# Two pairs of the third attention summed unit by unit on VectorE, and its softmax sums joined without TensorE

## The chip, the cores and the metric

The kernel runs on one core of a Trainium2 chip. The metric is the device time of one execution in microseconds.

## The reference

The computation is a grouped-query attention over 8 batches (16 query heads, 4 key heads, 384 positions, head size 64), whose output goes through a hierarchical mixture of experts (4 groups of 4 experts, model width 1024, hidden width 1024). Cut to what matters:

```python
scores = scale * q @ k.T                       # per batch and head, 384 x 384
attn = exp(scores - max); attn /= attn.sum(-1) + 1e-9
x = (attn @ v) laid out as 3072 tokens x 1024
g = argmax(x @ w_group);  e = argmax(x @ w_expert[g])     # one expert per token
out = softmax_g[g] * softmax_e[e] * (relu(x @ w1[g, e]) @ w2[g, e])
```

## The kernel before

Each batch is one attention followed by one block. An attention has 24 units (4 groups of heads, 6 units of keys each). For unit u, TensorE makes the scores (L318), ScalarE their exponentials into a tile e of 128x768 (L324), and TensorE multiplies these with v into PSUM (L337), two units behind the scores. The result of a group is copied to xT by VectorE (L379).

The softmax sums are made beside that. GpSimd adds the tiles of two units (`pair`, L345), in place in the first of them, and VectorE reduces the sum with a transposing reduction (`reduce`, L354). `lags` says at which unit's tail a reduction is queued; in the third attention (b = 2) the reduction of pair u-2 stands in the tail of unit u, and the last one, of unit 23, in the block behind it. A unit in `apart` is not added: `pair` does nothing and `reduce` reduces both tiles, each into a slot of its own of `red3`. The list of the third attention is empty before.

The block behind an attention interleaves the expert layer of the batch before (`moe_h` L636, `ffn_y` L650) with the end of the softmax. `join_keys` adds the slots of each group: with equal numbers of slots it is one instruction (L407), otherwise one for each group. Then the sums of the 32-row strips must be added and spread over the partitions. There are two ways: `sums` does it with TensorE (L416) and two reciprocals on VectorE (L432); `sums_copied` does it on VectorE alone, with copies and additions (L441, L442), one reciprocal (L443) and eight copies (L447). The third batch uses `sums`, those after it `sums_copied`. Then `normalise` runs four times, each a transposing spread (L455) and a multiplication (L459). Behind that VectorE casts a small mean (L482), and TensorE makes the gate's logits (L474), the softmax of the gate follows, and the next attention.

In the block of b = 2 VectorE also runs the gate's softmax of batch 1 (L505 to L537) and its output weights (L614, L618), between `join_keys` and the sums. On GpSimd the same block queues a wait for the transposed q (L604), two weight loads, and three additions that sum v (L112 to L114).

Every engine works off its queue in the order of the program, which is written out by hand.

Of the kernel before, what the change touches and what calls it, by code (L numbers as in the profile page):

```python
# [18 lines left out]
def kernel(  # L19
# [14 lines left out]
    _, Hkv, _, _ = k.shape  # L34
# [12 lines left out]
    NU = Hkv * NC  # L47
# [20 lines left out]
    def ps_tile(which, shape=None, dtype=F32):  # L68
        if which == "x":
            which = f"o{1 - turn['o']}"  # L70
        else:
            turn[which] = 1 - turn[which]
            which += str(turn[which])
        return psum.tile(shape or [P, 2, 512], dtype, name="ps_" + which)
# [20 lines left out]
    def load_k(b, src=None):  # L95
        nc.gpsimd.dma_start(out=k_pad[:, D:(NK + 1) * D].rearrange("p (a n) -> p a n", n=NC * D),
                            in_=rows(k[b] if src is None else src))

    def load_q(b, src=None):
        qraw[b] = lpool.tile([P, KQ, NC * D], BF16, name="q_raw")  # L100
        nc.gpsimd.dma_start(out=qraw[b], in_=rows(q[b] if src is None else src))

    def load_v(b, src=None):
        vraw[b] = vpool.tile([P, NA, NC * D], F32, name="v_raw")
        nc.sync.dma_start(out=vraw[b], in_=rows(v[b] if src is None else src))

    def sum_v(b):
        t = gpool.tile([P, NA * D], BF16, name="vsum")
        s = gpool.tile([P, NA, NC // 2 * D], F32, name="vs")
        v_ = vraw[b]  # L110
        hn = NC // 2 * D
        nc.gpsimd.tensor_add(out=s, in0=v_[:, :, :hn], in1=v_[:, :, hn:])  # L112
        nc.gpsimd.tensor_add(out=s[:, :, :D], in0=s[:, :, :D], in1=s[:, :, D:2 * D])
        nc.gpsimd.tensor_add(out=t.rearrange("p (h d) -> p h d", d=D), in0=s[:, :, :D],  # L114
                             in1=s[:, :, 2 * D:])
        vsum[b] = t
# [285 lines left out]
    def join_keys(b, g0, g1):  # L402
        if b not in red:
            red[b] = gpool.tile([P, Hkv, 2, NB], F32, name="red", bufs=2)
        same = len(set(parts[b][g0:g1])) == 1
        for g, h in [(g0, g1)] if same else [(g, g + 1) for g in range(g0, g1)]:
            nc.vector.tensor_reduce(  # L407
                out=red[b][:, g:h].rearrange("p g t j -> p g (t j)"),
                in_=red3[b][:, g:h, :parts[b][g]].rearrange("p g c t j -> p g (t j) c"),
                axis=AX.X, op=ALU.add)  # L410

    def sums(b, g0, g1, which, tiles=False):
        sm = ps_tile(which)[:, :, :(g1 - g0) * 2 * NB]
        for r in range(2):
            if not tiles:
                nc.tensor.matmul(out=sm[:, r], lhsT=half32[:, r, :],  # L416
                                 rhs=red[b][:, g0:g1].rearrange("p g t j -> p (g t j)"),
                                 start=True, stop=True)
                continue
            rs = slice(r * H2, (r + 1) * H2)  # L420
            for t in range(2):
                nc.tensor.matmul(
                    out=sm[t * D:(t + 1) * D, r].rearrange("p (g t j) -> p g t j", t=2, j=NB)[:, :, t],
                    lhsT=half32[rs, r, t * D:(t + 1) * D], rhs=red[b][rs, g0:g1, t],
                    start=True, stop=True)
        if b not in inv:
            inv[b] = gpool.tile([P, KQ, NB], F32, name="inv", bufs=2)
        iv = inv[b][:, 2 * g0:2 * g1].rearrange("p (g r) j -> p r g j", r=2)
        sm = sm.rearrange("p r (g t j) -> p r g t j", t=2, j=NB)
        for t in range(2):  # L430
            ts = slice(t * D, (t + 1) * D)
            nc.vector.reciprocal(out=iv[ts], in_=sm[ts, :, :, t])  # L432
# [3 lines left out]
    def sums_copied(b, which):  # L436
        r_, sm = red[b], red3[b][:2 * Q, :, 4]
        sw = ps_tile(which)[:, 0, :Hkv * 2 * NB].rearrange("p (g t j) -> p g t j", t=2, j=NB)
        for r in range(2):
            lo, hi = slice(2 * r * Q, (2 * r + 1) * Q), slice((2 * r + 1) * Q, (2 * r + 2) * Q)  # L440
            nc.vector.tensor_copy(out=sw[lo], in_=r_[hi])  # L441
            nc.vector.tensor_add(out=sm[r * Q:(r + 1) * Q], in0=r_[lo], in1=sw[lo])  # L442
        nc.vector.reciprocal(out=sm, in_=sm)  # L443
        inv[b] = gpool.tile([P, KQ, NB], F32, name="inv", bufs=2)
        for r in range(2):
            for h in range(4):
                nc.vector.tensor_copy(out=inv[b][h * Q:(h + 1) * Q, r::2, :],  # L447
                                      in_=sm[r * Q:(r + 1) * Q, :, h // 2, :])
# [157 lines left out]
    def pick_w1(b):  # L606
        w1s[b] = fetch1(ers[b])
# [37 lines left out]
    def ffn_y(w2, hT, c, which, nhs=(0, 1), y=None):  # L645
        if y is None:
            y = ps_tile(which)
        for nh in nhs:
            for f in range(FQ):
                nc.tensor.matmul(out=y[:, nh, :], lhsT=hT[:, f, c * P:(c + 1) * P],  # L650
                                 rhs=w2[:, f, nh * HALF:(nh + 1) * HALF],
                                 start=(f == 0), stop=(f == FQ - 1))
        return y
# [19 lines left out]
    def moe_y(b, c, which):  # L673
        y_out(b, c, ffn_y(w2s[b], hTs[b], c, which))
# [6 lines left out]
    def before_attention(b):  # L681

        if b + 1 < B:
# [10 lines left out]
             for i in range(5)]  # L694
    at = {
        0: Attn(0, act_copies=(0, 1, 3),
                lags={5: [1], 6: [3], 8: [5], 10: [7], 12: [9], 14: [11], 18: [13], 21: [15],
                      22: [17]}),
        1: Attn(1, apart=(9, 11), act_copies=(2, 3), later=(7, 13, 15, 17), homes=homes,
                lags={18: [13], 19: [15], 20: [17], 22: [19], 23: [21]}),  # L700
    }
# [97 lines left out]
    def first_block():  # L799
        load_v(3)  # L800
        moe_y(0, 0, "s")
        sum_v(2)
        load_k(3)
        load_q(3)
        at[1].reduce(NU - 1)
        join_keys(1, 0, Hkv)
        y = ffn_y(w2s[0], hTs[0], 1, "s", (0,))
        sums(1, 0, Hkv, "o")
        ffn_y(w2s[0], hTs[0], 1, "s", (1,), y)
        y_out(0, 1, y)  # L810
        y = ps_tile("o")
        normalise(1, 0, "x")
        normalise(1, 2, "x")
        cast(1, 0)
        ffn_y(w2s[0], hTs[0], 2, "o", (0,), y)
        at[2] = Attn(2, later=(1,), lags={5: [1], 6: [3], **{u: [u - 2] for u in range(7, NU, 2)}})
        at[2].score(0)
        at[2].score(1)
        ffn_y(w2s[0], hTs[0], 2, "o", (1,), y)
        y_out(0, 2, y)  # L820
        normalise(1, 1, None, pool)
        normalise(1, 3, None, pool)
# [17 lines left out]
    def block(b):  # L840
        last = b == B - 1
        f = b - 1
        if b + 2 < B:
            load_v(b + 2)
        if not last:
            after_transposes(b + 1)
        pick_w1(b)
        pick_w2(b)
        if not last:
            sum_v(b + 1)  # L850
        if b + 2 < B:
            load_k(b + 2)
            load_q(b + 2)
        moe_h(f, 0, "s")
        at[b].reduce(NU - 1)
        join_keys(b, 0, Hkv)
        if b == 2:
            gate_softmax(1, state["gl"], False)()
            out_weights(1)
        moe_h(f, 2, "s")  # L860
        if b == 2:
            sums(b, 0, Hkv, "o")
        else:
            sums_copied(b, "o")
        normalise(b, 0)
        normalise(b, 1)
        moe_h(f, 4, "s")
        normalise(b, 2)
        moe_h(f, 6, "s")
        cast(b, 0)  # L870
        cast(b, 1)
        normalise(b, 3)
        moe_y(f, 0, "s")
        cast(b, 2)
        pt = ps_tile("o")
        y = ffn_y(w2s[f], hTs[f], 1, "s", (0,))
        vm = None if last else guess_mean(b + 1, pt)
        ffn_y(w2s[f], hTs[f], 1, "s", (1,), y)
        cast(b, 3)
        y_out(f, 1, y)  # L880
        gate_logits(b, pt)
        if not last:
            guess_logits(vm, guess_out(pt))
            at[b + 1] = Attn(b + 1)
            at[b + 1].score(0)
            at[b + 1].score(1)
        w = gate_softmax(b, gate_rows(pt, not last), not last)
        if not last:
            pick(b + 1)
            pick_index(b + 1)  # L890
            read_pick(b + 1)
        w()
        out_weights(b)
        y = ffn_y(w2s[f], hTs[f], 2, "o")
        if last:
            y_out(f, 2, y)
            return {}
        return {1: [do(y_out, f, 2, y, True)]}
# [148 lines left out]
```

## Time and profile before

| what | value |
|---|---|
| median of 3 runs | 359.56 us (358.8 to 362.1) |
| the profiled execution's own time | 359.14 us |
| its span | 357.2 us |
| TensorE busy (matmul) | 347.3 us, 97% |
| VectorE busy | 256.6 us, 72% |
| ScalarE busy | 225.1 us, 63% |
| GpSimd busy | 220.4 us, 62% |

The span is what the trace covers; the own time is 1.9 us longer. Times in the trace are microseconds from the span's start. The third attention runs from 73.5 to 95.6 us, its block to 119.4 us.

### The profile page before, as it was taken

What the parts mean: (1) busy time and instruction counts of PE and PEld (TensorE: products, weight loads), DVE (VectorE), ACT (ScalarE), POOL (GpSimd) and SP (SyncE); (2) the same over time, 40 slices, a digit from 0 to 9 for tenths busy, and PEclk for the clock granted to TensorE, in tenths of its full rate; (3) what the DMA queues carried; (4) which work ended last, traced back from release to release, by engine and by line L of the source; (5) the groups of instructions that cost most, each with busy time, mean ns of one, the idle gap of its engine ahead of it and who ended that gap; (6) DMA issues with size and microseconds to landing.
All of it is one profiled execution on the core that took longest, in us unless ns stands there. A gap on an engine that the chain in (4) does not pass through costs nothing.

```text
span 357.2 us, 9201 instructions
## 1 busy us (share of the span) xinstructions
PE 347.3 (97%) x3799; PEld 183.1 (51%) x3814; DVE 256.6 (72%) x521; ACT 225.1 (63%) x295; POOL 220.4 (62%) x172
## 2 busy tenths in 40 slices
PE   8999999999999999999999999999999999999993
PEld 4455565445555455544555554545545544555642
DVE  5797769767697777977679767886769676795031
ACT  5899935399536794378934598256963679444320
POOL 6879995869935598607984099902995059900000
PEclk9999999999999999999999999999999999999999
DMA  8999999799999999899989999899987991099924
GB/s 203 185 157 163 222 208 177 130 272 223 194 173 178 262 208 188 190 221 244 193 199 177 233 226 194 180 204 250 196 182 124 197 267 65 2 183 220 245 67 117
DMA packets 69486, 67.15 MB, mean 188 GB/s; under 512 B 37144, under 2 KB 49688, under 8 KB 69440
## 3 DMA queue, kind: packets, MB, share of 16 engines
q0 software_dynamic: 26640, 41.03, 66.3%
q1 hardware_dynamic: 42352, 24.94, 30.3%
q8 instruction: 32, 0.52, 0.6%
q10 hardware_dynamic: 448, 0.54, 0.5%
q14 instruction: 14, 0.11, 0.1%
HBM read 86.07 MB, written 12.58 MB: 276 GB/s over the span
## 4 chain that ended last, share of the span: by engine, by line
PE 83%; DVE 6%; POOL 5%; ACT 2%; issue 1%; POOLq 0%; DVEq 0%
PE ps_o L337 29%; PE ps_s L636 19%; PE ps_s L650 11%; PE ps_s L318 8%; PE ps_o L650 6%; PE ps_o L474 3%; POOL e L345 2%; ACT e L324 2%; PE ps_s L927 2%; POOL w L345 1%; PE ps_o L636 1%; DVE xT L459 1%; PE ps_o L927 1%; DVE e L455 1%; POOL xb L466 1%
## 5 line engine op out<-in xcount | busy, mean ns | idle before, releaser
L345 POOL TENSOR_TENSOR e<-e 128x768 f32<-128x768 f32 x91 | 162.7, 1825 | 74.6 <-PE ps_s L318 67.9
L324 ACT ACTIVATE e<-ps_s 128x768 f32<-128x768 f32 x187 | 147.6, 813 | 19.5 <-PE ps_s L318 17.4
L337 PE MATMUL ps_o<-e,v_raw 64*64 64x384 f32 x1496 | 149.1, 482 | 0.0
L354 DVE TRANSPOSE_TENSOR_REDUCE red<-e 128x24 f32<-128x768 f32 x95 | 91.4, 971 | 38.1 <-POOL e L345 38.1
L636 PE MATMUL ps_s<-xb,w 128*128 128x384 bf16 x480 | 80.1, 326 | 0.1
L337 PEld LDWEIGHTS ps_o<-e,v_raw 64*64 64x64 f32 x1496 | 55.3, 133 | 36.4 <-issue 29.0
L636 PEld LDWEIGHTS <-w 128*128 128x128 bf16 x512 | 49.4, 98 | 36.4 <-issue 4.5
L318 PE MATMUL ps_s<-qT,kT 64*64 64x384 bf16 x768 | 64.7, 328 | 0.3
L650 PEld LDWEIGHTS <-hT 128*128 128x128 bf16 x336 | 31.8, 98 | 38.8 <-issue 2.3
L640 ACT ACTIVATE hT<-ps_s 128x768 bf16<-128x768 f32 x23 | 18.6, 810 | 50.6 <-PE ps_s L636 47.2
L650 PE MATMUL ps_s<-w,hT 128*128 128x512 bf16 x217 | 49.4, 379 | 0.4
L318 PEld LDWEIGHTS <-kT 64*64 64x64 bf16 x768 | 24.3, 105 | 34.6 <-issue 32.6
L464 ACT CAST xb<-xT 128x768 bf16<-128x768 f32 x28 | 23.3, 832 | 10.0 <-DVE xT L459 9.8
L379 DVE COPY xT<-ps_o 128x768 f32<-128x768 f32 x26 | 24.0, 924 | 2.6 <-ACT xb L464 1.5
L455 DVE STREAM_TRANSPOSE e<-inv 128x768 f32<-128x768 f32 x26 | 25.2, 971 | 0.2
L650 PE MATMUL ps_o<-w,hT 128*128 128x512 bf16 x105 | 24.0, 379 | 1.1 <-issue 1.1
L459 DVE TENSOR_TENSOR xT<-xT,e 128x768 f32<-128x768 f32 x24 | 23.1, 961 | 0.8
L669 ACT ACTIVATE ot<-ps_s,we 128x1024 f32<-128x1024 f32 x14 | 15.6, 1114 | 8.6 <-PE ps_s L650 8.5
L495 DVE STREAM_TRANSPOSE gl<-ps_o 128x96 f32<-128x96 f32 x8 | 2.3, 283 | 16.8 <-PE ps_o L487 12.2
L643 ACT ACTIVATE hT<-ps_s 128x384 bf16<-128x384 f32 x14 | 6.1, 488 | 12.5 <-PE ps_s L636 12.5
L447 DVE COPY inv<-red 32x48 f32<-32x48 f32 x40 | 10.6, 265 | 0.6
L474 PEld LDWEIGHTS ps_o<-xT,wg 128*32 128x32 f32 x448 | 9.2, 110 | 3.7 <-DVE vm L482 1.7
(141 smaller groups left out, 227.3 us busy)
## 6 DMA issues: line engine op xcount, KB each, us to landing
w<-in_moe_w_dram POOLq DMA_DIRECT2D x16, 2048.0 KB, 21.9
out_dram<-ot SPq DMA_DIRECT2D x42, 256.0 KB, 7.1
q_raw<-in_q_dram POOLq DMA_DIRECT2D x7, 768.0 KB, 27.4
v_raw<-in_v_dram SPq DMA_DIRECT2D x7, 384.0 KB, 4.6
k_raw<-in_k_dram POOLq DMA_DIRECT2D x7, 192.0 KB, 24.4
out_dram<-ot SPq DMA_DIRECT2D x9, 128.0 KB, 2.7
w<-in_q_dram POOLq DMA_DIRECT2D x3, 192.0 KB, 6.3
w<-in_k_dram SPq DMA_DIRECT2D x2, 192.0 KB, 3.7
```

The source lines that it names most:

```text
L318: nc.tensor.matmul(out=sT[r * H2:(r + 1) * H2, s, :S], lhsT=kT[b][s * D:(s + 1) * D, key_block(b, s, g // 2, c), ks], rhs=qT[b][s * D:(s + ...
L324: nc.scalar.activation(e.rearrange("p t (s x) -> p s t x", s=2), sT[:, :, :S].rearrange("p s (t x) -> p s t x", t=2), ACT.Exp, scale=scale)
L337: nc.tensor.matmul(out=oT[t * D:(t + 1) * D, r, :S], lhsT=vraw[b][r * H2:(r + 1) * H2, g // 2, c * D:(c + 1) * D], rhs=self.e[u][r * H2:(r ...
L345: nc.gpsimd.tensor_add(out=self.e[u - 1], in0=self.e[u - 1], in1=self.e[u])
L354: nc.vector.tensor_reduce(out=red3[b][:, g, parts[b][g]].rearrange("p t j -> p (t j)"), in_=self.e[w].rearrange("p t (j x) -> p (t j) x", ...
L379: nc.vector.tensor_copy(out=dst, in_=src)
L455: nc.vector.transpose(out=rb.rearrange("p k (j x) -> p k j x", x=32), in_=inv[b][:, ks].unsqueeze(3).to_broadcast([P, 2, NB, 32]))
L459: eng.tensor_mul(out=x, in0=x, in1=rb)
L464: nc.scalar.copy(out=xb[b][:, ks, :], in_=xT[b][:, ks, :])
L474: nc.tensor.matmul(out=pt[32 * t:32 * t + 32, 0, :S // 4], lhsT=wg[:, head_pair(m), :], rhs=x[:, t], start=(m == 0), stop=(m == KQ - 1))
L636: nc.tensor.matmul(out=h[:, jj, :S], lhsT=w1[:, head_pair(m), (f0 + jj) * P:(f0 + jj + 1) * P], rhs=x[:, m, :], start=(m == 0), stop=(m == ...
L650: nc.tensor.matmul(out=y[:, nh, :], lhsT=hT[:, f, c * P:(c + 1) * P], rhs=w2[:, f, nh * HALF:(nh + 1) * HALF], start=(f == 0), stop=(f == ...
```

## The change

Two things change, both for b = 2. The pairs that end in units 15 and 21 get into `apart`: GpSimd doesn't add them, VectorE reduces their four tiles one by one, and two of the four groups then have four slots in `red3` in place of three. And the block no longer calls `sums` for b = 2 but `sums_copied`, as for the later batches.

```diff
-        at[2] = Attn(2, later=(1,), lags={5: [1], 6: [3], **{u: [u - 2] for u in range(7, NU, 2)}})
+        at[2] = Attn(2, apart=(15, 21), later=(1,), lags={5: [1], 6: [3], **{u: [u - 2] for u in range(7, NU, 2)}})
...
         moe_h(f, 2, "s")
-        if b == 2:
-            sums(b, 0, Hkv, "o")
-        else:
-            sums_copied(b, "o")
+        sums_copied(b, "o")
         normalise(b, 0)
```

## Rows read from the trace of the kernel before

**Rows 1.** The page: busy time of each engine, share of the span.
```profile
PE 347.3 (97%) x3799; PEld 183.1 (51%) x3814; DVE 256.6 (72%) x521; ACT 225.1 (63%) x295; POOL 220.4 (62%) x172
```

**Rows 2.** The chain that ended last, 90 to 165 us: start, length, what.
```profile
93.67 1.94 PE ps_o L337 x24
...
100.93 0.69 PE ps_o L416 x4
...
112.00 1.75 PE ps_s L650 x8
113.74 1.46 PE ps_o L474 x64
...
145.80 1.05 DVE inv L447
...
156.02 0.17 DVE vm L482
```

**Rows 3.** Timeline of TensorE, the gate's logits of the third and the fourth batch.
```profile
113.67 1.53 PE L474 MATMUL ps_o<-xT,wg 128*32 128x96 f32 x64
...
156.23 1.53 PE L474 MATMUL ps_o<-xT,wg 128*32 128x96 f32 x64 [0.27 <-DVE vm L482]
```

**Rows 4.** Timeline of VectorE, 80 to 114 us: start, length, instruction [idle before].
```profile
83.77 2.69 DVE L354 TRANSPOSE_TENSOR_REDUCE red<-e 128x24 f32<-128x768 f32 x3
...
90.51 0.98 DVE L354 TRANSPOSE_TENSOR_REDUCE red<-e 128x24 f32<-128x768 f32 x1 [0.81 <-POOL e L345]
92.28 0.98 DVE L354 TRANSPOSE_TENSOR_REDUCE red<-e 128x24 f32<-128x768 f32 x1 [0.80 <-POOL e L345]
93.18 0.92 DVE L379 COPY xT<-ps_o 128x768 f32<-128x768 f32 x1
94.07 0.98 DVE L354 TRANSPOSE_TENSOR_REDUCE red<-e 128x24 f32<-128x768 f32 x1
...
99.38 0.98 DVE L354 TRANSPOSE_TENSOR_REDUCE red<-e 128x24 f32<-128x768 f32 x1
100.39 0.48 DVE L407 TENSOR_REDUCE red<-red 128x96 f32<-128x288 f32 x1
100.79 0.15 DVE L505 TENSOR_REDUCE mx<-gl 128x3 f32<-128x12 f32 x1
...
103.86 1.51 DVE L432 RECIPROCAL inv<-ps_o 64x96 f32<-64x96 f32 x2
105.41 0.98 DVE L455 STREAM_TRANSPOSE e<-inv 128x768 f32<-128x768 f32 x1
...
113.12 0.16 DVE L482 CAST vm<-ps_o 128x2 bf16<-128x2 f32 x1
```

**Rows 5.** Timeline of GpSimd, 64 to 110 us.
```profile
77.95 21.39 POOL L345 TENSOR_TENSOR e<-e 128x768 f32<-128x768 f32 x12
104.33 0.18 POOL L604 COPY tok<-qT 1x1 bf16<-1x1 bf16 x1 [4.99 <-DMA qT<-q_raw]
...
106.76 1.54 POOL L112 TENSOR_TENSOR vs<-v_raw 128x384 f32<-128x384 f32 x1
```

**Rows 6.** Groups by form, `join_keys`: busy, mean ns of one, idle before.
```profile
L407 DVE TENSOR_REDUCE red<-red 128x96 f32<-128x288 f32 x6 | 2.9, 478 | 0.2
...
L407 DVE TENSOR_REDUCE red<-red 128x24 f32<-128x72 f32 x5 | 1.0, 213 | 0.0
```

**Rows 7.** Timeline of VectorE, 309 to 328 us, the last batch's `sums_copied`.
```profile
312.72 0.25 DVE L441 COPY ps_o<-red 32x96 f32<-32x96 f32 x1
...
314.64 1.52 DVE L447 COPY inv<-red 32x48 f32<-32x48 f32 x8
316.20 0.98 DVE L455 STREAM_TRANSPOSE e<-inv 128x768 f32<-128x768 f32 x1
```

**Rows 8.** Timeline of VectorE and of GpSimd, 134 to 162 us, the fourth batch.
```profile
145.36 2.98 DVE L447 COPY inv<-red 32x48 f32<-32x48 f32 x8
...
145.79 1.02 POOL L112 TENSOR_TENSOR vs<-v_raw 128x384 f32<-128x384 f32 x1
```

## The prediction, made before the changed kernel ran

> **What bounds the kernel now.** I read the page first: TensorE is busy for 97% of the span, no other engine for more than 72% [rows 1]. So a change to VectorE and GpSimd counts only where TensorE waits for them, or where it takes instructions off TensorE. Then I read the chain of waits from the third attention to the fifth. In the block that is changed it never leaves TensorE: the attention's last products, 32 matmuls of the expert layer, the four L416 matmuls of `sums` (0.69 us), the expert layer again, and at 113.74 the gate's logits, which begin the moment that the matmuls in front of them end [rows 2]. One block later it does leave TensorE: there the logits wait for VectorE's small cast L482 and start 0.04 us behind its end (156.02 + 0.17, then 156.23), a wait of 0.27 us [rows 2, 3]. This pair, L482 and L474, is where VectorE can stop TensorE: L482 stands behind all four `normalise` in VectorE's queue, and the logits write the PSUM tile that it reads.
>
> So the question is how much room VectorE has in front of L482 in the third block. L482 ends at 113.28, the logits start at 113.67 by TensorE's timeline and 113.74 by the chain [rows 2, 3, 4]: 0.4 us of room. The rest is a sum along VectorE's queue.
>
> **TensorE: less work.** The four L416 matmuls go. They lie on the chain with nothing beside them, so TensorE is ready for the logits 0.69 us earlier, at 113.05 [rows 2].
>
> **GpSimd: two additions fewer.** It runs 12 of them back to back in 21.39 us, 1.78 each, to 99.34 [rows 5]. Nothing before the pair of unit 15 changes, and VectorE's reduction of unit 13 still waits for GpSimd until 90.51 [rows 4]. From there GpSimd adds pairs 17 and 19 (to about 94.05), and pair 23 as soon as unit 22 has been multiplied; the last three units' products take from 93.67 to 95.61, so unit 22 is done at about 94.96 [rows 2]. Pair 23 is ready at about 97.1 instead of 99.34. GpSimd itself wins nothing by it: its next instruction waits for a DMA until 104.33 [rows 5], which the change does not touch, and the block's additions for v keep their place at 106.76.
>
> **VectorE in the attention.** From 90.51 before, five reductions, two copies and three waits of 0.8 us for GpSimd (two lie further down than the row shown) led to the last reduction at 99.38 and the join at 100.39 [rows 4]. After, the waits are gone and two reductions are added. Start to start, a reduction behind a reduction takes 0.88 (three in 2.69, the last 0.94 long), a reduction before a copy 0.90, a copy before a reduction 0.89, and the last one 1.01 until the join [rows 4]. The queue is units 13, 14, 15, copy, 17, 19, 20, 21, copy, 23: 5 x 0.88 + 2 x 0.90 + 2 x 0.89 + 1.01 = 8.99, so the join starts at 99.50, 0.9 us earlier. Pair 23 (97.1) is then no limit, since its reduction starts at 98.5; VectorE's own work is.
>
> **The join.** Groups with three slots and with four no longer go in one instruction. One of 128x288 was followed by the next instruction after 0.40 us [rows 4]. Now there are two of 128x72 (213 ns) and two of 128x96, by the line through the two forms (478 - 213) / 216 = 1.23 ns an element, 243 ns [rows 6]. With 20 ns of overlap each that is 0.82 us, 0.42 more. Bounds: 0.8 if all overlap, 0.95 if none does. The gate's softmax that follows starts at 100.3 instead of 100.79 and keeps its 3.07 us (100.79 to 103.86) [rows 4]. VectorE is 0.5 us ahead there.
>
> **The sums.** Before: two reciprocals, 103.86 to 105.41, 1.55 us [rows 4]. After: thirteen instructions. Their price is seen in later batches that already run them: the last one takes 312.72 to 316.20, 3.48 us [rows 7], the fourth takes 1.46 more, since its eight copies need 2.98 us in place of 1.52 [rows 7, 8]. So 1.93 to 3.39 us are added. The end of the fourth batch's copies shows why: one of them takes 1.05 us, from 145.80 to 146.85 [rows 2], exactly while GpSimd adds v (145.79 to 146.81) [rows 8]; the others are 0.18 to 0.35. In the third block the copies would run from 103.35 + 1.92 = 105.3 to 106.8, and the addition for v starts at 106.76 [rows 5]: the last copy starts some 0.2 us ahead of it. I take the cheap price and keep the dear one as a rival. [...]
>
> **Sum for the block.** VectorE: -0.9 + 0.4 + 1.9 = +1.4 us, so L482 ends at 113.28 + 1.4 = 114.7 and the logits start at 114.75, against 113.67 before: TensorE is 1.1 us later, although it was ready 0.6 us sooner than before. It stands idle for about 1.7 us there. Of this wait 0.69 is the gain of the dropped matmuls, used up.
>
> **After the block** everything hangs on TensorE and shifts with it, with one exception: in the fourth block GpSimd's additions for v hang on a DMA wait that doesn't shift, while VectorE's copies do. They start at 145.36 + 1.1 = 146.5 instead of 145.36, when most of the addition that blocked them (to 146.81) is over [rows 8]. So the fourth block's chain on VectorE gets some 0.6 us shorter and its wait of 0.27 us on TensorE goes. Bounds: 0 to 0.27 given back. The later blocks' logits start with the matmuls ahead of them, and keep to TensorE.
>
> Net +1.1 - 0.3 = +0.8 us. On the profiled execution's 359.14 that is 359.95; on the median of the three runs (359.56, which is 0.4 above the profiled one) it is 360.4. I put the forecast between, 360.2.
>
> **Rivals.**
> *The copies collide with GpSimd in the third block.* The mechanism is that of the fourth batch, at L447 and L112; it decides if VectorE reaches the copies a few tenths of a microsecond later than worked out (a dearer join, or reductions at 0.98), or if GpSimd reaches L112 earlier. One copy held costs about 0.9, all three additions 1.46 [rows 7, 8]; TensorE is then 2.0 to 2.6 us later in this block, net 361 to 362 and slower than before. [...] Against it: by my sum the last copy starts first.
> *VectorE is covered and TensorE keeps its gain.* That needs L482 to end by 113.05, that is VectorE's sum to come out at -0.2 instead of +1.4. It would need the reductions to overlap more, or the attention's part to start before 90.51. Then 359.14 - 0.69 = 358.5, by the median 358.9; half of it, 359.3 to 359.7. For it: the whole chain on TensorE in rows 2. Against it: thirteen instructions for two, each priced by a row.
> *The change does not free VectorE from GpSimd.* If pair 23 still came at 99.3, the 0.9 us would be lost, TensorE would be 2.0 us later, 361.2. Against it: GpSimd has two additions fewer in its queue and idle time behind.
>
> **How the numbers follow.** Forecast (net 0.3 to 1.4 us more on either base, 359.4 to 361.0): 0.55. Collision or late pair 23 (361 to 362.2): 0.22. Covered (358.5 to 359.5): 0.18. Something with a larger effect, such as a lower granted clock of TensorE behind the idle 1.7 us, which no row here can show: 0.05. The range takes in the first three, on either base: 358.6 to 362.2. About 1%, 3.6 us, is what a measurement of this kernel can tell from no change; all three cases are inside it. So 0.95 for within 1%, 0.04 for slower, 0.01 for faster.
>
> **What would show it.** In the profile after: no L416 in this block; 89 additions L345 of the e form instead of 91; the join at about 99.5 in four pieces; the first L455 at about 106.8; L482 at 114.5; a wait on TensorE of 1.5 to 2 us for L482 in front of L474 at about 114.8; L447 of the fourth block shorter than 2.98. Wrong would be: logits that start at 113.0 (covered), an L447 of about 1 us in the third block (collision), or any other stretch than these two blocks that changes its length.

## The result and the profile after

The changed kernel takes 361.74 us in the median of 22 runs (359.06 to 364.1), the kernel before 359.08 us in 22 runs. The ratio is 1.0071, with a 95% interval from 1.0056 to 1.0086: 2.5 us slower by the ratio (2.7 between the medians). That is within the 1% that was given 0.95, at the upper end of the range, and above the likeliest case (359.4 to 361.0); the interval is much narrower than the 1% that the prediction took for what can be told from no change. The rival in which VectorE's copies collide with GpSimd came true, though with other instructions of GpSimd than it named, and with it the fall of TensorE's clock that had been put among the remaining 0.05.

The page of the changed kernel, busy times and the granted clock in 40 slices, has one slice besides the last, at the kernel's end, in which the clock is not full, about 117 to 126 us:

```profile
PE 348.1 (97%) x3795; PEld 183.9 (51%) x3810; DVE 261.9 (73%) x537; ACT 224.8 (62%) x295; POOL 216.2 (60%) x170
...
PEclk9999999999999899999999999999999999999998
```

In this execution all that comes before the third attention is already 0.6 us later than in the trace before: TensorE waited 0.6 us at 11 us, at a place that the change does not touch. So times are compared below from the end of the third attention on, 95.61 us before [rows 2] and 96.25 after.

The chain that ended last, of the changed kernel, in the third block (start, length, what):

```profile
106.71 0.18 DVE inv L447
...
106.90 1.43 DVE inv L447
...
116.00 0.17 DVE vm L482
...
116.21 2.78 PE ps_o L474 x64
...
119.15 0.72 PE ps_s L318 x7
```

The chain now goes through VectorE. Seven of the eight copies take 0.18 us, the eighth 1.43. The logits L474 start behind the cast L482 and take 2.78 us where they took 1.53 [rows 3]. VectorE's timeline shows how it got there:

```profile
91.13 2.70 DVE L354 TRANSPOSE_TENSOR_REDUCE red<-e 128x24 f32<-128x768 f32 x3 [0.81 <-POOL e L345]
...
99.77 0.78 DVE L407 TENSOR_REDUCE red<-red 128x24 f32<-128x72 f32 x4
100.47 0.15 DVE L505 TENSOR_REDUCE mx<-gl 128x3 f32<-128x12 f32 x1
...
103.64 0.25 DVE L441 COPY ps_o<-red 32x96 f32<-32x96 f32 x1
...
105.56 2.76 DVE L447 COPY inv<-red 32x48 f32<-32x48 f32 x8
108.35 0.98 DVE L455 STREAM_TRANSPOSE e<-inv 128x768 f32<-128x768 f32 x1
```

Behind 91.13 VectorE waits for none of GpSimd's pairs. (A merged line names the first form only: two of the four L407 have 128x96.) From the attention's end, the join starts at 3.52 us where it started at 4.78 [rows 2, 4], 1.26 us earlier; the gate's softmax 0.96 us earlier; the first L455 comes 2.30 us later (12.10 against 9.80). GpSimd's timeline, in the same stretch, tells what held the last copy:

```profile
95.78 1.81 POOL L345 TENSOR_TENSOR e<-e 128x768 f32<-128x768 f32 x1 [1.07 <-PE ps_o L337]
105.90 0.18 POOL L604 COPY tok<-qT 1x1 bf16<-1x1 bf16 x1 [8.30 <-DMA qT<-q_raw]
106.50 0.94 POOL L546 DMA_DIRECT2D w<-in_moe_w_dram  x1 [0.42 <-issue]
107.42 0.88 POOL L552 DMA_DIRECT2D w<-in_moe_w_dram  x1
108.31 1.01 POOL L112 TENSOR_TENSOR vs<-v_raw 128x384 f32<-128x384 f32 x1
```

The copy that started at 106.90 ended at 108.33, when the second of the two weight loads had been issued (107.42 + 0.88 = 108.30). It wasn't the addition for v, which held a copy for 1.05 us in the fourth batch before [rows 2, 8]; that one starts only now. TensorE's timeline and the windows behind it (length, busy of PE, PEld, DVE, ACT, POOL with counts, granted clock, DMA share, GB/s) show the rest:

```profile
116.21 2.78 PE L474 MATMUL ps_o<-xT,wg 128*32 128x96 f32 x64 [2.53 <-DVE vm L482]
```
```profile
113.60:116.20 2.60, 0.08 (x1) 0.00 (x0) 2.49 (x4) 1.51 (x3) 0.00 (x0) 1.00 1.12 210
116.20:120.00 3.80, 3.66 (x74) 2.87 (x76) 0.70 (x5) 1.92 (x3) 0.00 (x0) 0.55 1.04 199
120.00:123.30 3.30, 3.27 (x15) 1.37 (x14) 2.82 (x17) 1.45 (x3) 0.00 (x0) 1.00 1.10 292
```

TensorE idles for 2.53 us, is granted 0.55 of its full clock over the next 3.8 us, and 1.00 again from 120. From the attention's end, the logits start 1.90 us later than before (19.96 against 18.06 [rows 2, 3]), and the next attention's first products 3.44 us later (27.47 against 24.03), so the slow clock cost 1.54 us (3.44 - 1.90). In the fourth block the small wait of before [rows 3] is gone, which gives 0.33 us back. Nothing later differs by more than 0.3 us.

### The profile page after: what moved, and what is told of

The parts are those of the page before. It is cut to its first block, busy times and chain, and to the rows that moved or that the text cites. A ratio compares the mean times of both kernels' runs of the same rounds, so it can differ in the third digit from the quotient of the medians.

```text
span 360.6 us, 9203 instructions
## 1 busy us (share of the span) xinstructions
PE 348.1 (97%) x3795; PEld 183.9 (51%) x3810; DVE 261.9 (73%) x537; ACT 224.8 (62%) x295; POOL 216.2 (60%) x170
## 4 chain that ended last, share of the span: by engine, by line
PE 79%; DVE 9%; POOL 4%; ACT 3%; issue 3%; POOLq 0%; ACTq 0%
PE ps_o L337 26%; PE ps_s L636 19%; PE ps_s L650 11%; PE ps_s L318 8%; PE ps_o L650 6%; PE ps_o L474 3%; DVE red L354 2%; ACT e L324 2%; PE ps_s L924 2%; POOL w L345 1%; PE ps_o L636 1%; POOL e L345 1%; DVE xT L459 1%; PE ps_o L924 1%; DVE e L455 1%
## 5 line engine op out<-in xcount | busy, mean ns | idle before, releaser
L345 POOL TENSOR_TENSOR e<-e 128x768 f32<-128x768 f32 x89 | 159.2, 1818 | 80.9 <-PE ps_s L318 74.0
L354 DVE TRANSPOSE_TENSOR_REDUCE red<-e 128x24 f32<-128x768 f32 x97 | 92.7, 969 | 35.8 <-POOL e L345 35.8
L455 DVE STREAM_TRANSPOSE e<-inv 128x768 f32<-128x768 f32 x26 | 25.2, 971 | 0.2
L474 PE MATMUL ps_o<-xT,wg 128*32 128x96 f32 x448 | 11.9, 264 | 2.6 <-DVE vm L482 2.5
L474 PEld LDWEIGHTS ps_o<-xT,wg 128*32 128x32 f32 x448 | 10.3, 118 | 5.9 <-DVE vm L482 3.4
## 6 DMA issues: line engine op xcount, KB each, us to landing
w<-in_moe_w_dram POOLq DMA_DIRECT2D x16, 2048.0 KB, 21.9
```

Of the source, the lines that this page charges most:

```text
L345: nc.gpsimd.tensor_add(out=self.e[u - 1], in0=self.e[u - 1], in1=self.e[u])
L354: nc.vector.tensor_reduce(out=red3[b][:, g, parts[b][g]].rearrange("p t j -> p (t j)"), in_=self.e[w].rearrange("p t (j x) -> p (t j) x", ...
L455: nc.vector.transpose(out=rb.rearrange("p k (j x) -> p k j x", x=32), in_=inv[b][:, ks].unsqueeze(3).to_broadcast([P, 2, NB, 32]))
L474: nc.tensor.matmul(out=pt[32 * t:32 * t + 32, 0, :S // 4], lhsT=wg[:, head_pair(m), :], rhs=x[:, t], start=(m == 0), stop=(m == KQ - 1))
```

## The experiments

Each kernel was timed against the kernel before in the same rounds; `apart_busy` ran only once.

**The two halves apart.** `apart_only` keeps `sums`, `copied_only` keeps the pairs whole:

```diff
 apart_only, against the kernel before:
+        at[2] = Attn(2, apart=(15, 21), later=(1,), ...)
 copied_only, against the kernel before:
-        if b == 2:
-            sums(b, 0, Hkv, "o")
-        else:
-            sums_copied(b, "o")
+        sums_copied(b, "o")
```

> The first half of the change alone: the two pairs are reduced unit by unit on VectorE, the sums stay with TensorE. Theory (the apart pairs help VectorE, the copied sums cost): the join starts 1.2 us earlier as in the changed kernel, the small cast L482 ends about 0.9 us earlier, the logits L474 don't wait for it, and the time is that of the kernel before within 0.3 us. Rival (the two added reductions are what makes VectorE late): a wait in front of L474 of over 1 us and 1.5 to 3 us more than before.

> The second half alone: the sums are copied on VectorE, no pair is apart. Theory: the copies start 0.9 us later than in the changed kernel, as the join does, the cast L482 ends 2.3 us or more later than before, TensorE waits 3 us or more in front of L474 and runs behind that at a low granted clock; 3 to 4.5 us more than before, so slower than the changed kernel by 0.5 to 1.5 us. Rival (the apart pairs are the cost): faster than the changed kernel, within 1 us of before.

`apart_only`: 359.56 us against 359.16, ratio 1.0010 (0.9999 to 1.0021); the theory's 0.3 us lies inside the interval. `copied_only`: 364.79 us, ratio 1.0140 (1.0118 to 1.0162), 5 us slower and more than either theory gave. So the copied sums are the cost, and the apart pairs take half of it back. TensorE's and VectorE's timelines of `copied_only`:

```profile
117.32 2.79 PE L474 MATMUL ps_o<-xT,wg 128*32 128x96 f32 x64 [4.09 <-DVE vm L482]
```
```profile
106.04 3.38 DVE L447 COPY inv<-red 32x48 f32<-32x48 f32 x8
```

From the attention's end the join comes 1.25 us later than in the changed kernel, the copies meet both the weight loads and the additions for v (3.38 us for eight), and behind 4.09 us of idle time the clock is low for longer: 0.50 is granted from 117 to 121 us and 0.71 from 121 to 125.

In `apart_only` the third block has no wait, but the profile shows a longer one than before [rows 3] in the fourth:

```profile
145.05 4.04 DVE L447 COPY inv<-red 32x48 f32<-32x48 f32 x8
```
```profile
156.98 1.53 PE L474 MATMUL ps_o<-xT,wg 128*32 128x96 f32 x64 [1.29 <-DVE vm L482]
```

The fourth block's copies are held for 2.5 us of their 4.04, since GpSimd's work in that block starts 1.1 us later than before (L604 at 144.52 in place of 143.39), while VectorE's does not.

The third block of `apart_only` got 0.3 us shorter, although L416 stays (logits 17.79 us behind the attention's end, 18.06 before). TensorE's weight loads show why, in the kernel before and in `apart_only`:

```profile
100.92 0.52 PEld L416 LDWEIGHTS ps_o<-red,half 128*128 128x128 f32 x4 [0.40 <-DVE red L407]
```
```profile
100.58 0.58 PEld L416 LDWEIGHTS ps_o<-red,half 128*128 128x128 f32 x4
```

Before, the weights of L416 came from VectorE's join L407 and waited 0.40 us for it; with the earlier join they don't.

**The clock.** `filled` is the changed kernel with the eight matmuls ahead of the third block's logits done twice:

```diff
         ffn_y(w2s[f], hTs[f], 1, "s", (1,), y)
+        if b == 2:
+            ffn_y(w2s[f], hTs[f], 1, "s", (1,), y)
```

> The changed kernel, with the last eight matmuls in front of the logits of the third block done twice (the same sums into the same place, 1.75 us), so that TensorE is idle for 0.8 us instead of 2.5. Theory (the idle time drops TensorE's clock, and that costs about 1.5 us on top of the wait): the granted clock stays at its higher level, the 64 L474 take 1.5 us and not 2.8, the wait for L482 ends when it did; 1.3 to 1.8 us less than the changed kernel in the median, and a narrower spread of times. Rival (the clock falls for another reason, or it costs nothing since VectorE is late again behind it): the same time as the changed kernel, or slower.

360.59 us, ratio 1.0038 (1.0021 to 1.0055): 1.15 us below the changed kernel's median (a little less than the 1.3 to 1.8 expected), with 1.75 us more work on TensorE. The times lie between 359.76 and 361.44; the changed kernel's span 5 us. The logits in its profile:

```profile
115.43 1.53 PE L474 MATMUL ps_o<-xT,wg 128*32 128x96 f32 x64 [0.83 <-DVE vm L482]
```

The cast L482 ends when it did, 19.94 us behind the attention's end (115.37 and 95.43; 19.91 in the changed kernel), and the 64 matmuls take 1.53 us again. So without most of the idle time the clock does not fall here: 1.00 is granted from 113 to 125 us.

**The held copy.** `from_psum` is the changed kernel in which the third block's eight copies read PSUM:

```diff
-        nc.vector.reciprocal(out=sm, in_=sm)
+        if b == 2:
+            nc.vector.reciprocal(out=sw[:2 * Q], in_=sm)
+            sm = sw[:2 * Q]
+        else:
+            nc.vector.reciprocal(out=sm, in_=sm)
```

> The changed kernel, but in the third block the reciprocal is written to PSUM and the eight copies L447 read it there, so that they have no SBUF input. Theory (one copy was held by GpSimd's weight-load issues): none of the eight is longer than 0.4 us, the first L455 starts about 1.0 to 1.2 us earlier against the join, the wait in front of L474 is 1.2 to 1.5 us instead of 2.5; 1 to 2.5 us less than the changed kernel, the more if the clock then stays up. Rival (the long copy was late for another reason, such as a wait for data): it stays long and the time the same.

360.30 us, ratio 1.0025 (1.0011 to 1.0039): 1.4 us below the changed kernel, although its GpSimd issues the same two loads in that stretch. VectorE's timeline (the added lines shift the numbers by four: L451 are the copies, L463 the multiplication):

```profile
104.94 1.69 DVE L451 COPY inv<-ps_o 32x48 f32<-32x48 f32 x8
...
107.68 1.67 DVE L463 TENSOR_TENSOR xT<-xT,e 128x768 f32<-128x768 f32 x1
```

No copy is held. But in this execution, the slowest of its 12, the first multiplication, which reads two tiles, takes 1.67 us in place of 0.96, beside the addition for v at 107.51. The wait in front of the logits was then 2.17 us and not the 1.2 to 1.5 that was expected: part of the hold had moved one instruction on. And the clock fell in this execution too, granted 0.57 from 116 to 120 us:

```profile
116.00:120.00 4.00, 4.00 (x55) 1.76 (x45) 2.57 (x14) 2.58 (x4) 0.00 (x0) 0.57 1.06 219
```

**Moving VectorE's work away.** Three kernels run the gate's softmax of the second batch, 3 us in the third block, inside the third attention, at units 9 and 15: `early_copied` with the copied sums alone, `early_both` with both halves, `early_psum` as the first with all copies out of PSUM.

```diff
+    def second_softmax():
+        state["w1"] = gate_softmax(1, state["gl"], False)
+
+    def second_weights():
+        state["w1"]()
+        out_weights(1)
...
+        9: [second_softmax],
+        15: [second_weights],
...
-        if b == 2:
-            gate_softmax(1, state["gl"], False)()
-            out_weights(1)
```

> The copied sums without apart pairs, and the gate's softmax of the second batch, 3.1 us of VectorE, moved out of the third block into the third attention (units 9 and 15), where VectorE waits for GpSimd's pairs five times, 3.7 us together. Theory (only VectorE's work between the join and the cast L482 makes TensorE wait; without it the dropped L416 matmuls are a gain): the copies run before GpSimd's weight loads, L482 ends near 112.2, before TensorE is ready for the logits, no wait there, and the time is 0.5 to 1 us below the kernel before. Rival (the softmax only moves the delay into the attention, where the reductions and the join come later by as much): the join comes 2 to 3 us later and the time is 1 us or more above before.

> The changed kernel with the same move of the gate's softmax. Theory: VectorE has fewer waits to fill in this attention, so the join comes 1.5 to 2 us later than in the changed kernel and the copies start 1 to 1.5 us earlier; they miss GpSimd's weight loads, L482 ends 2 to 2.5 us earlier, the wait in front of L474 is 0 to 0.6 us and the clock stays up: 2 to 3 us below the changed kernel, within 0.7 us of before. Rival (the wait stays, as the join comes 3 us later): as slow as the changed kernel.

> The kernel with copied sums, early softmax and no apart pairs, and in all batches the reciprocal goes to PSUM and the eight copies read it there. Theory (the copies of the fourth batch are held by GpSimd's additions for v, and that alone makes TensorE wait 0.3 us there): no copy is over 0.3 us in any block, the wait of the fourth block is gone, and the time is 0 to 0.4 us below the kernel with early softmax alone. Rival (the hold only moves on to the multiplications L459, which read two tiles): no gain, or slower.

All three are far slower: 365.60, 363.89 and 365.45 us, ratios 1.0171 (1.0147 to 1.0195), 1.0132 (1.0109 to 1.0154) and 1.0186 (1.016 to 1.0212). The theory failed at the price of the moved work. VectorE's, GpSimd's and TensorE's timelines of `early_copied`, in the attention:

```profile
87.39 1.75 DVE L511 TENSOR_SCALAR ohg<-sh 128x12 f32<-128x12 f32 x1
89.17 1.78 DVE L513 TENSOR_TENSOR pr<-gl,ohg 128x48 f32<-128x48 f32 x1
```
```profile
78.39 16.02 POOL L345 TENSOR_TENSOR e<-e 128x768 f32<-128x768 f32 x9
```
```profile
93.68 0.36 PE L318 MATMUL ps_s<-qT,kT 64*64 64x384 bf16 x4 [2.16 <-ACT e L324]
96.46 0.92 PE L337 MATMUL ps_o<-e,v_raw 64*64 64x384 f32 x4 [2.43 <-DVE xT L379]
```

Instructions that take 0.17 and 0.21 us in the block take 1.75 and 1.78 here: each ends when one of GpSimd's back-to-back additions, 1.78 us long, has ended. The first half of the softmax took 7.9 us instead of 1.9; ScalarE's exponential for it, which waited 2.53 us for VectorE, held up the attention's, and TensorE waited twice. Behind these waits the clock fell inside the attention, granted 0.50 from 97 to 101 us (the window of `early_copied`, then the logits of `early_both`):

```profile
97.00:101.00 4.00, 4.00 (x33) 1.56 (x28) 3.83 (x9) 1.62 (x2) 1.80 (x1) 0.50 1.17 165
```
```profile
119.47 1.53 PE L474 MATMUL ps_o<-xT,wg 128*32 128x96 f32 x64 [1.22 <-DVE vm L482]
```

The attention ended 29.3 us after its first products in place of 21.9. In the third block of `early_copied` the logits have no wait, as the theory said, but not for its reason: the copies run at 109.47, behind GpSimd's weight loads (105.33 to 107.14) and not ahead of them. In `early_both` a wait of 1.22 us stays, more than the 0 to 0.6 that was expected, as the join comes 2.6 us later than in the changed kernel. In `early_psum` no copy is longer than 0.25 us, and no time is won by it: TensorE waits in none of these blocks of `early_copied` either.

**GpSimd's start in the block.** `apart_busy` is the changed kernel in which GpSimd still adds the apart pairs, into tiles that nobody reads.

> The changed kernel, but GpSimd still makes the two additions of the apart pairs, into spare tiles that nobody reads. It looks at why the wait for the transposed q ends 6.5 us after the transpose is issued in the kernels with apart pairs, 5.5 us in those without. Theory (GpSimd's earlier idle time has to do with it): 5.5 us, and the copies meet the additions for v rather than the weight loads. Rival (it has not): 6.5 us, as in the changed kernel.

SyncE's issue of the transposed q and the end of GpSimd's wait for it, in `apart_busy`:

```profile
99.13 3.64 SPq L147 DMA_TRANSPOSE qT<-q_raw  x1
```
```profile
104.71 0.18 POOL L607 COPY tok<-qT 1x1 bf16<-1x1 bf16 x1 [4.95 <-DMA qT<-q_raw]
```

5.6 us, as in the kernel before, in `copied_only`, and in `early_both`, whose GpSimd adds until 102.2 us; it is 6.5 in the changed kernel (99.36, 105.90) and 6.5 to 6.7 in the three others above that have apart pairs and an idle GpSimd. The copies met both the weight loads and the additions for v (3.20 us for eight), and the time of this one run, 365.17 us, goes with a wait of 3.99 us in front of the logits. Why the wait ends later when GpSimd has been idle for longer is not shown.

**Useful work in the wait.** `split` is the changed kernel with the first half of the block's last output ahead of the logits; `split_psum` has the copies of the third block out of PSUM as well; `split_all` has both edits in all blocks from the third to the seventh; `before_split` has both edits in these blocks on the kernel before. (In the last two the first line is `split = not last`.)

```diff
         y_out(f, 1, y)
+        split = b == 2
+        if split:
+            y = ffn_y(w2s[f], hTs[f], 2, "o", (0,))
         gate_logits(b, pt)
...
-        y = ffn_y(w2s[f], hTs[f], 2, "o")
+        y = ffn_y(w2s[f], hTs[f], 2, "o", (1,) if split else (0, 1), y if split else None)
```

> The changed kernel, but in the third block eight of the sixteen matmuls that follow the logits are done in front of them (the first half of the last expert output), 1.75 us of work that is needed anyway. Theory (only the idle time in front of the logits and the clock behind it cost): the wait for L482 is 0.5 to 0.9 us, the clock stays up, and behind the logits 1.75 us less is left to do: 2.5 to 3.5 us below the changed kernel's 361.7, that is 0 to 0.7 us below the kernel before. Rival (the later logits make VectorE's gate softmax late, and the next attention pays for it): 1 us or more above before.

> The same, and the eight copies of the third block read the reciprocal in PSUM, where GpSimd doesn't hold them. Theory: the wait is 0.5 us or less, 0.2 to 0.8 us below the kernel with the split alone, 0.3 to 1 us below the kernel before. Rival (the multiplications L459 are held instead): no difference from the split alone.

> Both edits in every block from the third to the seventh. Theory (the fourth block's small wait goes too, the others have none): equal to the kernel with both edits in the third block, or up to 0.4 us below. Rival (the logits of the later blocks, which have no wait, come 1.75 us later and VectorE's work behind them with them): slower than that kernel by 0.5 us or more.

> The kernel before (no apart pairs, the third batch's sums by TensorE) with both edits of the fastest kernel in every block from the third to the seventh: half of the last output in front of the logits, the eight copies out of PSUM. Theory (the change's one gain is the 0.69 us of L416, kept where nothing waits): only the fourth block's wait of 0.27 us goes, 0.1 to 0.4 us below before, and 0.3 to 0.9 us above the kernel that has the change and both edits (ratio 0.9981 of before). Rival (the change gives nothing, all of that gain is from the two edits): the same ratio as that kernel, 0.998 or below.

| kernel | us | ratio to before | interval |
|---|---|---|---|
| `split` | 359.85 | 1.0020 | 1.0009 to 1.0031 |
| `split_psum` | 360.17 | 1.0028 | 1.0016 to 1.0040 |
| `split_all` | 358.29 | 0.9981 | 0.9966 to 0.9995 |
| `before_split` | 358.67 | 0.9977 | 0.9962 to 0.9991 |

`split` won 1.9 us back and missed its range by a little: it stayed above the kernel before. `split_psum` has no wait in the third block, but was not faster than `split`, against its theory. TensorE's timeline of `split`, third and fourth block, and of `split_psum`, fourth block (its lines are shifted by four):

```profile
115.44 1.53 PE L474 MATMUL ps_o<-xT,wg 128*32 128x96 f32 x64 [0.83 <-DVE vm L482]
...
156.97 1.53 PE L474 MATMUL ps_o<-xT,wg 128*32 128x96 f32 x64 [0.95 <-DVE vm L482]
```
```profile
156.71 1.53 PE L478 MATMUL ps_o<-xT,wg 128*32 128x96 f32 x64 [1.39 <-DVE vm L486]
```

In the changed kernel and these two, the sooner the third block ends, the longer is the wait in the fourth: 0, 0.95, 1.39 us. GpSimd's work in that block comes sooner too, but by less than VectorE's: the fourth block's join starts 1.09 us behind L604 in the changed kernel (147.01 and 145.92), 0.19 ahead of it in `split` (143.94 and 144.13) and 0.63 ahead in `split_psum` (143.24 and 143.87), and in these two L604 waits for the transposed q again. The fifth block has a wait of 0.62 and 0.65 us then. With both edits in every block the fourth and the fifth have none, and `split_all` is the fastest of the kernels with the change, by its ratio 0.7 us below before and by more below `split_psum` than its theory gave. TensorE's timeline of `split_all` (lines shifted by one):

```profile
114.98 1.53 PE L475 MATMUL ps_o<-xT,wg 128*32 128x96 f32 x64 [0.48 <-DVE vm L483]
...
157.21 1.53 PE L475 MATMUL ps_o<-xT,wg 128*32 128x96 f32 x64
```

But `before_split`, without the change, is as fast, so the rival of that run held: the change itself gives nothing that these runs can tell from zero, even where its waits are covered; the intervals leave room for some 0.5 us either way. The two profiles fit: of what the third block wins without L416, 0.48 us still go into its wait, and the next attention's first products come 0.16 us sooner than in `before_split` (23.71 and 23.87 us behind the attention's end). The apart pairs with `sums` kept and both edits, which would keep the 0.3 us of `apart_only`, were not run.

## Why the prediction was right in its range and too low in size

**TensorE: less work.** Right in size: L416 is gone, and the matmuls up to the logits end 0.7 us sooner from the attention's end. But these are two gains. L416 did not only lie on TensorE's queue, it waited there for VectorE's join, which the matmul rows of the chain don't show and the weight loads do. `apart_only` gets 0.3 of the 0.7 us with L416 in place; dropping it is worth the other 0.4. That the chain never leaves TensorE in this block, with which the prediction began, was thus too strong.

**VectorE in the attention and the join.** Right in mechanism, a little better in size: the join starts 1.26 us earlier and not 0.9 (the steps of the queue are some hundredths shorter, a reduction behind a reduction 0.86 us rather than 0.88, and the last one takes 0.88 to the join rather than 1.01), the softmax 0.96 and not 0.5. The rival that GpSimd still sets the last reduction fell: pair 23 was ready at 97.6, its reduction started at 98.9. `apart_only` shows this half without a cost in its own block, but with a longer wait in the next.

**The sums.** This is the term that was mis-sized. It was taken at 3.48 us, the price of the last batch [rows 7], and measured 4.71 (103.64 to 108.35), near the dear case of 4.94, which was chosen against by 0.2 us of clearance. The sign that was named for it, an L447 of about 1 us in the third block, came: 1.43. That clearance was worked out from GpSimd's instructions of before, and two things in it were wrong. First, not only the additions for v hold a copy: the weight loads that GpSimd issues ahead of them do too, and the prediction passed over them: in its own times the copies (105.3 to 106.8) lie beside both issues. GpSimd's timeline of the kernel before, third and fourth block, and the first of the fourth batch's copies in the chain:

```profile
104.94 0.94 POOL L546 DMA_DIRECT2D w<-in_moe_w_dram  x1 [0.42 <-issue]
105.87 0.88 POOL L552 DMA_DIRECT2D w<-in_moe_w_dram  x1
...
144.90 0.88 POOL L552 DMA_DIRECT2D w<-in_moe_w_dram  x1
```
```profile
145.36 0.43 DVE inv L447
```

The trace before had the sign: of the 2.98 us [rows 8] the first copy took 0.43, and it ended with that issue (145.78). Second, "its next instruction waits for a DMA until 104.33, which the change does not touch" was wrong by 0.9 us: the wait ended at 105.90, 9.65 us behind the attention's end and not 8.72 [rows 2, 5], and `apart_busy` shows that GpSimd's freed time goes with it. What this second error cost is not shown; with the wait at its old place, in `copied_only`, the copies met more of GpSimd's work and not less. `from_psum` shows the hold itself: with copies that read PSUM it was gone (1.69 us for the eight), and 1.4 us of the loss with it, a part of it through the clock, whose mean is 0.995 or more in 11 of its 12 runs. The holds were not all alike. The copy that started behind an addition ended with it (1.05 us [rows 2, 8]), and nearly so the two-tile multiplication in `from_psum` (0.71 us more, with 0.84 of the addition left). Behind an issue only a part of the copies waited: those that started 0.02 and 0.21 us after the first issue were not held, the one that started 0.4 us after it was, until the second had ended. Why is not shown.

**The sum for the block.** Expected: logits 1.1 us later behind an idle 1.7 us. Measured: 1.90 later behind 2.53.

**The clock.** It had no term of its own, only a part of the last 0.05, since the trace before had no such idle time. It cost 1.54 us in the profiled execution, more than any other term was off. `filled` shows that the idle time did it: behind 0.83 us in place of 2.53 the logits took 1.53 us and not 2.78. It goes with the spread, too. Of the 22 runs of the changed kernel seven have a mean granted clock of 0.996 or more, and their median is 360.1 us; thirteen have 0.992 to 0.995, as the profiled execution (0.993), with a median of 362.1; the two slowest, 363.92 and 364.1, have 0.989. So about 1.1 us over the kernel before are there even where the clock, as far as its mean tells, stayed up, and the rest comes with its fall.

**After the block.** Right in effect: the fourth block's wait went (0.33 us with what hung on it, bounds 0 to 0.27), and its copies got shorter. GpSimd's wait did shift, though: the lines of the fourth block, L604 before, then L604 and the copies after:

```profile
143.39 0.18 POOL L604 COPY tok<-qT 1x1 bf16<-1x1 bf16 x1 [1.51 <-DMA qT<-q_raw]
```
```profile
145.92 0.18 POOL L604 COPY tok<-qT 1x1 bf16<-1x1 bf16 x1
```
```profile
149.45 2.12 DVE L447 COPY inv<-red 32x48 f32<-32x48 f32 x8
```

L604 no longer waits for the DMA but stands behind GpSimd's own additions, 1.9 us later from the third attention's end; the copies come 3.4 us later, with TensorE, and so start behind the first and longest of GpSimd's additions for v (L112, done at 149.33). The runs added what the prediction did not say: that wait is tied to how early the third block ends, so that a cure in one block comes back as a wait in the next (`apart_only`, `split`, `split_psum`).

In the profiled execution the terms close: 0.8 us forecast, 1.2 more for the sums, 1.5 for the clock, 0.5 less for the attention and the join make 3.0, against 3.44 - 0.33 = 3.1 measured from the third attention's end to the fifth's; the median moved by 2.5.

That the time fell into the range is in part luck. The range had no place for the clock, and the case that was given 361 to 362.2 was priced with logits 2.0 to 2.6 us later; they came 1.90 later, since the attention won 0.5 us more, and the clock added its 1.54. The 360.1 us of the seven runs with the highest clock agree with the forecast, 360.2, only because errors offset each other: the sums term was 1.2 us too small, the attention 0.5 better, and the base, 359.08 in 22 runs, lay 0.5 below that of the forecast.

Open is why GpSimd's wait for the transposed q ends later, and how long the wait in front of the logits is in the executions without a profile.

## What to carry to other kernels

Where VectorE is to take over work from TensorE, add up its queue to the instruction that TensorE waits for next; the room there (0.4 us here) is what the move may cost, not VectorE's idle share of 28%. Many small copies and two-input instructions were cheap only while GpSimd was quiet: eight copies took 1.52 us with GpSimd idle [rows 7] and up to 4.04 beside its issues and additions (`apart_only`), the two-tile multiplication 0.96 and, beside an addition, 1.67 us (`from_psum`). Price them at GpSimd's instruction length where the two overlap (here 0.88 to 0.94 us for a DMA issue, 1.01 to 1.54 for the first addition for v, 1.78 for one of L345), or let the copies read PSUM (1.69 us for eight beside the same two issues). A price is to be taken from a place where GpSimd does the same beside them. An idle stretch in front of TensorE was paid twice here, as a wait of 2.53 us and as 1.54 us for the slower clock behind it; useful matmuls moved into it took back 1.9 of the 2.5 us here, and then the next block's wait was the limit.

## What was not expected of the hardware

A VectorE copy of 32x48 waited for two DMA issues of GpSimd, 1.43 us in all, while copies that started 0.02 and 0.21 us after the first issue's start (106.52, 106.71) took their usual 0.18 us. Instructions of 12 and 48 elements a partition took 1.75 and 1.78 us beside GpSimd's additions, eight to ten times their usual time. And TensorE's clock fell behind idle times of 2.17 us (`from_psum`, granted 0.57 from 116 to 120 us), 2.53 us (the changed kernel, 0.55 from 116.2 to 120) and 4.09 us (`copied_only`, 0.50 from 117 to 121); behind 3.99 us in `apart_busy` the logits took 2.79 us. Behind the idle times of 0.83 to 1.39 us in the third and the fourth blocks of the other kernels they kept their 1.53 us.
